# A fused attention and feed-forward kernel: the first batch worked by pair of heads, and a new order of loads and steps in the first two blocks

## The chip, the cores and the metric

The kernel runs on one core of one Trainium2 chip. The metric is the device time of one execution in microseconds (us). The core has five instruction queues that run side by side: TensorE (PE, the matrix unit; its loads of weights into the array are listed as PEld), VectorE (DVE), ScalarE (ACT), GpSimd (POOL) and SyncE (SP). SP, ACT and POOL can also start DMA transfers; here SP and POOL start nearly all of them. Each queue works strictly in the order in which the program wrote it, and waits at an instruction until the semaphores that it needs have come.

## What is computed

The reference, cut to what matters (8 batches, 8 heads, 576 rows, 64 columns a head; then a feed-forward layer of 512 by 2048 by 512 over all 4608 rows):

```python
q_s = softmax(q, over the 64 columns)
k_s = softmax(k, over the 576 rows)
kv  = einsum('bhsd,bhde', k_s transposed, v)       # 64 x 64 a head
x   = einsum('bhsd,bhde->bhse', q_s, kv)           # rows of 512 = 8 heads x 64
h   = x @ w_in                                     # 512 -> 2048
g   = where(h > 0, h, exp(min(h, 0)) - 1)
out = g @ w_out                                    # 2048 -> 512
```

## The kernel before

The feed-forward layer is most of the work. It goes batch by batch (a *block* j, 0 to 7, of 512 of the batch's 576 rows; a ninth block holds the 64 rows left over of all batches), and in each block over 16 *steps* c, one for each 128 columns of the hidden layer. A step has four matmuls of the hidden product (line 912, one for each pair of heads kc), the ELU on ACT, POOL and DVE (lines 892 to 896 and 925), and four matmuls of the output product (line 933). The output product of a step comes three steps later (`LAG`). Both products take their weights from SBUF (`W1S`, `W2S`), into which POOL loads them piece by piece in the first block; a word `w2:6:9` loads chunks 6 to 8 of `w_out`.

Everything else is woven into this by hand. For batch 0 the list `START` is worked off before block 0 begins. For batches 1 and later the work of batch j+1 stands in the tables `FIRST` (during block 0), `SECOND` (block 1) and `LATER`. A table has for each step three strings of words: after the hidden product, after the output product, and after the ELU of that step. Each word appends instructions to the queues of its engines in this order, so the order of the words is the order in every queue. The words that matter here:

- `load:Q:0:1` loads a pair of heads (a slot of 288 KB) of q of batch 0; in `START` the last field may name the queue. `load:K:1:M` loads all four slots of k of the next batch.
- `kmax` (DVE, four instructions a slot, line 326), `kturn` (PE, 331), `kacross` (DVE, 337 or 358), `diag` (ACT, 368) find the column maxima of k. For batch 0 `kraw` (PE, 513) copies k into PSUM and `kmin` (PE, 524) subtracts the maximum there, and `kexp` (ACT, 538 and 533) takes the exponential from there. `kspread` and `copy` do for batch 1 what `kmin` does.
- `qmax` (DVE, 672), `qsub` (679), `qexp` (ACT, 684), `qsum` (DVE, 689 and 691) and `qmul` (708) make the softmax of q; `qsub` and `qmul` run on POOL unless the word says `dve`.
- `pturn` (PE, 766 or 744) transposes it into a PSUM bank and `pwide` (ACT, 788) copies it to `QT`.
- `vconv` converts v to bf16, `kv` (PE, 560) makes k's product with v, `kfac` (614 to 629) scales it into `MB`; `att` (PE, 805) makes a pair's rows of x, and `xc` (814 or 812) copies them to `XT`, from which the hidden product reads. From batch 2 on `flat` and `xflat` (827, 855) do this in six cuts.
- `h` in `START` starts part of the hidden product of steps 0 to 3 early; `warm` runs matmuls whose result nobody reads; `hold` makes SP wait for the hidden product.

`AT` says which of the eight PSUM banks each word of batch 0 uses. A word that writes a bank waits until its last reader is done. In the kernel before, the tail of batch 0 goes by halves: `qmul:A`, `pturn:A`, `kv:A` and so on are two pairs of heads at a time, and the first part of the hidden product can be started for pairs 0 and 1 alone, since `h` and line 888 split a step's four matmuls in two and two.

Of the kernel before, what the change touches and what calls it, by code (L numbers as in the profile page):

```python
# [15 lines left out]
R = 4  # L16
SM = 128 * R
# [103 lines left out]
class Gen:  # L121
# [421 lines left out]
    def vconv_first(self, part, en="act"):  # L543

        P = "AB".index(part)
        vv = self.VR[0][:, 2 * P * QN:2 * (P + 1) * QN, :].rearrange("p (u r) d -> p u r d", u=2)
        out = self.VF[:, :, 2 * P:2 * P + 2, 0:64].rearrange("p r s d -> p s r d")
        self.copy(en, out, vv, self.firstkeys("V", part), [f"VF{part}"])

    def kv_first(self, part, bank):  # L550

        pe, P = self.E["pe"], "AB".index(part)

        def mm():
# [653 lines left out]
```

## Time and profile before

| | |
|---|---|
| three runs | 309.95, 310.0, 309.95 us; median 309.95 |
| span of the profiled execution, first to last instruction | 308.1 us |
| median of the runs less this span | 1.85 us (309.95 - 308.1) |
| start of the first hidden product, of the first output product | 19.88 us, 24.47 us |
| start of block 1, of block 2 | 54.66 us, 87.78 us |
| granted TensorE clock, mean | 1.000 |

The profiled execution's own time is not listed apart from its span; what lies around the span is taken as the 1.85 us above. The profile is one execution; times in it are in microseconds from the first instruction. A row of the timeline has the start, the time to the end of the last of the merged instructions, engine, line of the kernel, operation, output and inputs, shapes, how many, and in square brackets how long the engine had been idle and what ended that. A row of the groups has the busy time of the group and the mean nanoseconds of one instruction, then the idle time before them. A row of the windows has a stretch and its length, and for each engine the busy time and the number of instructions. A row of the waits has who waited for whom, the sum, how often, and the longest.

### The profile page before, as it was taken

The page shows a single profiled execution, that of the slowest core. Times are in us where ns is not written, and L with a number is a line of the kernel's source. Part 1 is how long each engine was busy: PE and PEld are TensorE (multiplying, and loading weights), DVE is VectorE, ACT ScalarE, POOL GpSimd, SP SyncE. Part 2 cuts the span into 40 slices and gives each one's busy share as a digit, 9 for nine tenths or more (in the row PEclk, how much of TensorE's full clock was granted, in tenths as well). Part 3 has the DMA queues.
Part 4 walks back from the last instruction along what each step waited for, and adds up shares of the span by engine and source line. Part 5 has one row for each costly group of instructions (what it writes and reads, how often), then busy time and mean ns, then how long its engine had stood idle before and what let it go on. Part 6 is the DMA issues. An engine that isn't in the chain of part 4 may idle for free.

```text
span 308.1 us, 4839 instructions
## 1 busy us (share of the span) xinstructions
PE 297.6 (97%) x1733; PEld 240.1 (78%) x1733; DVE 235.0 (76%) x400; ACT 192.9 (63%) x358; POOL 171.3 (56%) x215
## 2 busy tenths in 40 slices
PE   7789899999999999999999999999999999999995
PEld 4467677788878888888888888888888888888884
DVE  6988978979959897999889988998895353335442
ACT  2678975577559784877587758775877543334432
POOL 2968873686436743786278637863686333333440
PEclk9999999999999999999999999999999999999999
DMA  7999999985708993768475846590512030003004
GB/s 261 393 340 364 372 345 257 273 253 145 191 3 246 261 251 105 223 122 231 133 217 144 208 143 209 146 198 3 172 23 57 2 136 0 0 2 136 0 0 136
DMA packets 60584, 51.63 MB, mean 168 GB/s; under 512 B 26897, under 2 KB 50705, under 8 KB 60561
## 3 DMA queue, kind: packets, MB, share of 16 engines
q1 hardware_dynamic: 52960, 41.23, 47.7%
q0 software_dynamic: 6400, 8.39, 10.5%
q10 hardware_dynamic: 1200, 1.72, 2.0%
q8 instruction: 13, 0.21, 0.3%
q14 instruction: 11, 0.08, 0.1%
HBM read 38.27 MB, written 9.45 MB: 155 GB/s over the span
## 4 chain that ended last, share of the span: by engine, by line
PE 85%; DMA 6%; POOL 4%; ACT 2%; DVE 2%; issue 1%
PE bank L933 40%; PE bank L912 40%; DMA W2S<-in_moe_w_out_dram 5%; PE bank L827 2%; POOL W1S L255 1%; PE bank L598 1%; DMA QR<-in_q_dram 1%; POOL QR L679 1%; POOL QS L708 1%; PE bank L805 1%; DVE KT L326 1%; DVE QF L672 0%; PE bank L560 0%; ACT ES L895 0%; ACT ES L893 0%
## 5 line engine op out<-in xcount | busy, mean ns | idle before, releaser
L933 PE MATMUL bank<-W2S,GT 128*128 128x512 f32 x572 | 153.4, 391 | 1.4 <-DMA W2S<-in_moe_w_out_dram 1.2
L896 POOL TENSOR_SCALAR ES<-ES 128x512 f32<-128x512 f32 (+1 forms) x130 | 85.8, 662 | 117.3 <-ACT ES L895 117.3
L912 PE MATMUL bank<-XT,W1S 128*128 128x512 f32 x512 | 138.4, 392 | 0.5 <-issue 0.3
L925 DVE SCALAR_TENSOR_TENSOR GT<-bank,ES 128x512 fp32r<-128x512 f32 (+1 forms) x130 | 87.9, 681 | 54.4 <-PE bank L912 40.6
L933 PEld LDWEIGHTS bank<-W2S,GT 128*128 128x128 f32 x572 | 106.3, 188 | 23.6 <-DMA W2S<-in_moe_w_out_dram 1.6
L895 ACT ACTIVATE ES<-bank 128x512 f32<-128x512 f32 (+1 forms) x130 | 76.0, 592 | 70.9 <-PE bank L912 70.7
L912 PEld LDWEIGHTS bank<-XT,W1S 128*128 128x128 f32 x512 | 94.1, 188 | 19.9 <-ACT XT L814 0.9
L679 POOL TENSOR_TENSOR QR<-QR,QM 128x512 f32<-128x512 f32 (+1 forms) x21 | 24.9, 1187 | 0.6 <-DVE QM L672 0.5
L684 ACT ACTIVATE QR<-QR 128x1024 f32<-128x1024 f32 (+3 forms) x19 | 19.0, 1006 | 3.1 <-DVE QR L679 3.1
L855 ACT ACTIVATE XT<-bank 128x320 fp32r<-128x320 f32 (+1 forms) x30 | 15.0, 501 | 9.4 <-PE bank L827 9.3
L689 DVE TENSOR_REDUCE QZ<-QR 128x16 f32<-128x1024 f32 (+1 forms) x14 | 18.8, 1343 | 0.6 <-ACT QR L684 0.6
L672 DVE TENSOR_REDUCE QM<-QR 128x16 f32<-128x1024 f32 (+1 forms) x14 | 18.8, 1342 | 0.0
L912 PE MATMUL bank<-XTR,W1S 128*128 128x512 f32 x64 | 16.6, 389 | 0.0
L438 DVE TENSOR_TENSOR KR<-KR,NB 128x512 f32<-128x512 f32 x16 | 14.6, 938 | 0.0
L623 ACT ACTIVATE MB<-bank,KZ 64x64 fp32r<-64x64 f32 x44 | 10.1, 302 | 7.0 <-DVE KZ L614 6.9
L387 DVE TRANSPOSE_TENSOR_REDUCE KM<-KR 128x32 f32<-128x1024 f32 x12 | 14.4, 1226 | 0.0
L857 POOL CAST QT<-QW 128x1024 fp32r<-128x1024 f16 x12 | 12.5, 1039 | 2.9 <-DMA QW<-QS 2.9
L912 PEld LDWEIGHTS bank<-XTR,W1S 128*128 128x128 f32 x64 | 12.0, 188 | 2.5
L892 ACT ACTIVATE ES<-bank 128x512 f32<-128x512 f32 x15 | 8.9, 594 | 7.9 <-PE bank L912 7.9
L827 PE MATMUL bank<-QT,MB 128*128 128x320 f32 (+1 forms) x48 | 12.5, 300 | 0.7 <-ACT XT L855 0.7
L708 POOL TENSOR_TENSOR QS<-QR,QI 128x1024 f16<-128x1024 f32 (+1 forms) x7 | 12.5, 1783 | 0.4 <-DVE QI L691 0.4
L484 ACT ACTIVATE EK<-KR 128x1024 bf16<-128x1024 f32 x12 | 12.6, 1050 | 0.0
(108 smaller groups left out, 262.8 us busy)
## 6 DMA issues: line engine op xcount, KB each, us to landing
out_dram<-OSB SPq DMA_DIRECT2D x30, 256.0 KB, 2.7
KR<-in_k_dram SPq DMA_DIRECT2D x6, 1024.0 KB, 7.7
VR<-in_v_dram SPq DMA_DIRECT2D x6, 1024.0 KB, 6.3
QR<-in_q_dram SPq DMA_DIRECT2D x5, 1024.0 KB, 8.0
KR<-in_k_dram SPq DMA_DIRECT2D x8, 288.0 KB, 6.1
VR<-in_v_dram SPq DMA_DIRECT2D x8, 288.0 KB, 6.6
W1S<-in_moe_w_in_dram POOLq DMA_DIRECT2D x3, 768.0 KB, 9.2
QR<-in_q_dram SPq DMA_DIRECT2D x4, 512.0 KB, 11.2
```

The costliest lines, as they stand in the source:

```text
L672: self.op("dve", lambda: v.tensor_reduce(m, QR, AX.X, ALU.max), self.qkeys(b, part), self.qstat("QM", b, part))
L679: self.op(en, lambda: e.tensor_tensor(QR, QR, m, ALU.subtract), keys + self.qstat("QM", b, part), self.qown(b, part))
L684: self.op("act", lambda: a.activation(QR, QR, AF.Exp), keys, self.qown(b, part))
L689: self.op("dve", lambda: v.tensor_reduce(z, QR, AX.X, ALU.add), self.qkeys(b, part), self.qstat("QZ", b, part))
L708: self.op(en, lambda: e.tensor_tensor(out, QR, z, ALU.mult), keys + self.qstat("QI", b, part), [f"QS{x}" for x in cells])
L827: last = pe.matmul(self.bank[bank][:, a - c0:b - c0], self.MB[f][:, :, :].rearrange("p u d -> p (u d)"), self.QT[:, f, a - f * S:b - f * S ...
L855: self.op("act", lambda: e.activation(out, src, AF.Copy), reads, writes)
L895: self.op("act", lambda: a.activation(ES[:, x], ps[:, x], AF.Exp), [f"bank{bank}"], keys + mark)
L896: self.op("gp", lambda: g.tensor_scalar(ES[:, x], ES[:, x], -1.0, 1.0, ALU.add, ALU.mult), keys, keys)
L912: return pe.matmul(ps, self.W1S[:, kc, c * 128:(c + 1) * 128], x[:, kc, 0:SM], start=(kc == 0), stop=(kc == 3))
L925: self.op("dve", lambda: v.scalar_tensor_tensor(out[:, x], *how), [f"bank{bank}"] + eks + (["FINE"] if n < FINE else []), keys)
L933: return pe.matmul(self.bank[OB[t]][:, :], self.GT[n % NG][:, t * 128:(t + 1) * 128], self.W2S[:, c, :], start=(c == 0), stop=(c == NCH - ...
```

## The change

Four things, in one edit.

1. From `qmul` on, batch 0 goes by single pair of heads. `vconv`, `kv`, `kfac`, `pturn`, `pwide` and the reads of `att` now take a slot number; each of the four `kv` and `pturn` has an entry of its own in `AT`, and `QT`, `KZ` and the converted v are tracked by slot. No instruction computes more or less; two-slot instructions become two of half the size.
2. The hidden product of steps 0 to 3 is written out matmul by matmul in `START`, so that each waits for one pair only, and block 0 begins with all of it issued.
3. `START`, `FIRST` and `SECOND` have a new order, and several words another engine. Of the loads, slot 3 of k and of q of batch 0 and then `w2:0:2` and `w1:0:4` are started by POOL at its beginning; v comes in the order 0, 1, 2, 3; the rows left over of q of batch 1 move from `START` to step 5, v of batch 1 from step 6 to step 10, k and q of batch 2 to step 11.
4. Of the eleven matmuls of `warm`, the first five stay.

```diff
-AT = {"rawA": 0, "rawA2": 1, "rawB": 7, "rawB2": 4, "rawS": 3, "rawT": 2,
-      "kturnA": 4, "kturnB": 5, "kvA": 6, "kvB": 4, "pturnA": 5, "pturnB": 5,
-      "att0": 6, "att1": 2, "att2": 3, "att3": 4, "clip": (1, 2, 4, 6, 8, 10, 11, 17, 21, 30, 32, 33, 37, 42, 44)}
-START = ("load:Q:0:1 load:K:0:0 load:K:0:1 warm:1:7 warm:4:7 qmax:1 warm:2:4 load:Q:0:3 qsub:1:dve "
-         "load:Q:0:0 kmax:0 warm:3:5 load:K:0:2 kraw:A qexp:1 kmax:1 load:K:0:3 kturn:A load:V:0:1 "
-         "qmax:0 kraw:S qsum:1 qsub:0:gp kacross:A load:Q:0:2 kmax:3 kraw:B kmax:2 kmax2:R "
-         "load:V:0:0 w1:1:4 w1:0:1 diag:act:A qmax:2 kmin:S qexp:0 kraw:T kturn:B w2:0:2 qmax:3 "
-         "w1:4:6 kacross:B kexp:S vconv:A:act kmin:A qsub:2:gp qsub:3:gp diag:act:B w2:2:3 qsum:0 kmin:B "
-         "kexp:A load:V:0:3 kmin:T qexp:2 qmul:A:dve qsum:2 load:V:0:2 qexp:3 w1:6:9 "
-         "qsum:3 vconv:B:gp load:K:1:M qmul:2:gp kexp:B kexp:T kv:A kfac:A:dve pturn:A kv:B "
-         "pwide:A:act kfac:B:act warm:1:3 att:1 att:0 qmul:3:gp pturn:B xc:1:dve xc:0 h:2:4 "
-         "pwide:B:act w2:3:4 att:2 att:3 xc:2 load:Q:1:A load:Q:1:R w2:4:6 h:0:2 xc:3 kmax2:AB ")
+AT = {"rawA": 3, "rawA2": 5, "rawB": 7, "rawB2": 1, "rawS": 7, "rawT": 5, "kturnA": 2, "kturnB": 6,
+      "kv0": 0, "kv1": 1, "kv2": 4, "kv3": 0, "pturn0": 6, "pturn1": 5, "pturn2": 7, "pturn3": 1,
+      "att0": 6, "att1": 3, "att2": 2, "att3": 4,
+      "clip": (1, 2, 4, 6, 8, 10, 11, 17, 21, 30, 32, 33, 37, 42, 44)}
+START = ("load:K:0:1 load:K:0:3:gp load:K:0:0 warm:5:2 kmax:1 load:Q:0:0 load:K:0:2 kmax:0 load:Q:0:2 qmax:0 kraw:A "
+         "kturn:A kraw:S load:Q:0:3:gp w2:0:2 kacross:A diag:act:A kmin:A load:Q:0:1 kmax:2 kexp:A load:V:0:0 "
+         "kmin:S kraw:T qmax:2 kmax:3 w1:0:4 qsub:2:gp kturn:B qmax:1 qsub:0:gp kacross:B kexp:S qexp:2 qexp:0 "
+         "diag:act:B kraw:B qmax:3 load:V:0:1 kmin:B qsub:1:gp vconv:0:gp qsum:0 kmin:T qsub:3:gp qexp:1 "
+         "vconv:1:act qsum:2 load:V:0:2 kv:0 qmul:2:gp qsum:1 qmul:1:gp qmul:0:dve kexp:B kfac:0:dve kv:1 "
+         "qexp:3 qsum:3 load:V:0:3 vconv:3:act load:K:1:M pturn:0 pturn:2 kexp:T kv:3 vconv:2:act w1:4:6 "
+         "pwide:0:act pturn:1 pwide:2:dve qmul:3:gp kfac:1:dve kv:2 pwide:1:act att:0 pturn:3 kfac:3:dve "
+         "xc:0:act att:1 pwide:3:act kfac:2:dve h:0:0:1 kmax2:AB w2:2:3 h:0:3:4 att:2 w2:3:4 att:3 xc:1:act "
+         "h:0:1:2 h:1:1:2 load:Q:1:A xc:2:act h:1:0:1 w1:6:9 h:0:2:3 h:2:0:1 xc:3:act h:3:0:1 h:1:2:3 h:2:1:2 "
+         "h:3:1:2 h:2:2:3 h:1:3:4 h:3:2:3 h:2:3:4 h:3:3:4 ")
 FIRST = {
-    0: ("qmax:A ksub:R:dve", "", "qsub:0:dve"),
-    1: ("w1:13:14", "w1:9:12", "qsub:1:dve"),
-    2: ("", "qmax0:R", "w2:6:9"),
-    3: ("hold qexp:A", "load:Q:1:B:act", ""),
-    4: ("w1:12:13", "w2:9:13", "load:K:1:R qsum:A qsub0:R:dve"),
-    5: ("w1:14:16", "kturn", "kacross vconv:R qmax:C"),
-    6: ("", "qmul:A hold", "load:V:1:RAB"),
-    7: ("qexp0:R", "", "diag qsub:2:dve"),
-    8: ("qsub:D", "kspread load:K:2:MR copy ksub:1 qsum0:R", "qexp:C qmulr0:dve ksub:0 qsum:C"),
-    9: ("pturn:A", "", "ksub:3 kexp:R qmul:B:dve pwide:A:act"),
-    10: ("", "pturn0:R pwide0:R:act", "ksub:2:dve vconv:A:gp"),
-    11: ("rest0 rcopy0:act", "kexp:A", ""),
-    12: ("pturn:B w2:15:16", "pwide:B:act load:Q:2:ABR", "w2:13:15"),
-    13: ("kv:A vconv:B:dve", "kfac:A:dve", "kexp:B peak2:B att:0 xc:0"),
-    14: ("kv:B kfac:B:dve peak2:R qmulr:gp", "att:1 peak2:A", "join2 turn:R xc:1"),
-    15: ("att:3", "xc:3", "att:2 load:V:2:MR xc:2 kout2"),
+    0: ("", "", ""),
+    1: ("w2:4:6 w1:9:12 qmax0:R", "", ""),
+    2: ("qmax:A w2:6:9", "", ""),
+    3: ("qsub:1:dve hold", "", ""),
+    4: ("", "load:Q:1:B:act qsub:0:gp", ""),
+    5: ("qexp:A w1:12:13 w2:9:13", "kturn load:Q:1:R kacross diag", ""),
+    6: ("", "qsum:A qmul:A:dve kspread", "copy qsub0:R:gp"),
+    7: ("w1:13:14 qexp0:R qsum0:R", "qmax:C qmulr0:gp pturn:A w1:14:16 qsub:D:dve", "pwide:A:act qsub:2:gp"),
+    8: ("", "ksub:0 pturn0:R", "pwide0:R:act qexp:C ksub:1:dve"),
+    9: ("rest0", "qsum:C", "hold"),
+    10: ("rcopy0:act qmulr:dve load:V:1:RAB turn:R", "kexp:A", "qmul:B:gp ksub:3:dve"),
+    11: ("load:K:2:MR load:Q:2:ABR ksub:2:dve vconv:A:gp", "", ""),
+    12: ("pturn:B", "pwide:B:act", "w2:15:16"),
+    13: ("kv:A kfac:A:dve", "w2:13:15 att:0 kexp:B vconv:B:dve xc:0", ""),
+    14: ("kv:B kfac:B:act", "att:1 peak2:B xc:1", ""),
+    15: ("att:2 peak2:A", "xc:2 att:3 load:V:2:MR xc:3 peak2:R", "join2 kout2"),
 }
 SECOND = {
-    0: ("qmax:C qsub:D", "", "qmax:A"),
-    1: ("", "qsub:1 wide0:R:dve", ""),
-    2: ("", "qsub:0 load:K:2:MR", ""),
-    3: ("kin", "qsub:2 qexp:A", "qsum:A vconv:A:gp"),
-    4: ("", "", "ksub:A"),
-    5: ("rest0", "qexp:C", "peak2:B"),
-    6: ("ksub:3:dve rcopy0:act vconv:B", "ksub:R:dve", "load:Q:2:MR"),
-    7: ("", "kexp:A", "ksub:2 kexp:R"),
-    8: ("qmul:1 qsum:C qmul:0:dve", "vconv:R", "kexp:B qmulr:dve"),
-    9: ("turn:A", "qmul:B:dve", ""),
-    10: ("peak2:R wide:A:gp kv:AB", "", ""),
-    11: ("kfac:AB:dve", "turn:R turn:B qmax2:A", ""),
-    12: ("peak2:A wide:R:act", "flat:0", "xflat:0:act"),
-    13: ("flat:1", "xflat:1:act", ""),
-    14: ("join2", "flat:2 xflat:2:act kout2", "wide:B:gp load:V:2:MR"),
-    15: ("flat:3", "xflat:3:dve flat:4", "xflat:4:act flat:5 xflat:5:act xrest:dve"),
+    0: ("qmax:A wide0:R:act qmax:C", "", "qsub:2"),
+    1: ("", "", "kin"),
+    2: ("load:K:2:MR", "", "qsub:0 ksub:2:dve"),
+    3: ("", "qsub:1 ksub:R:dve qsub:D:dve vconv:B", ""),
+    4: ("vconv:R", "", "qexp:A ksub:A qsum:A"),
+    5: ("peak2:A qexp:C ksub:3:gp", "", ""),
+    6: ("", "", "vconv:A:act qmul:0:gp"),
+    7: ("rest0", "kexp:B", "kexp:A qmul:1 qsum:C rcopy0:dve kexp:R qmulr:dve"),
+    8: ("", "load:Q:2:MR", ""),
+    9: ("peak2:B", "", ""),
+    10: ("load:V:2:MR kv:AB turn:A qmul:B:gp wide:A:act kfac:AB:act turn:R turn:B wide:R:act", "peak2:R", ""),
+    11: ("", "", "flat:0 xflat:0:act"),
+    12: ("", "qmax2:A", "flat:1 xflat:1:act"),
+    13: ("wide:B:dve", "flat:2", "xflat:2:act"),
+    14: ("flat:5 xflat:5:dve join2", "flat:3 xflat:3:act", ""),
+    15: ("flat:4", "xflat:4:act xrest:act kout2", ""),
 }
...
     def kv_first(self, part, bank):
-        pe, P = self.E["pe"], "AB".index(part)
+        pe, xs = self.E["pe"], self.slots(part)
...
-            for x in range(2 * P, 2 * P + 2):
+            for x in xs:
...
-        self.hidden_mm(j, c, range(2, 4) if n < EARLY else range(4))
+        self.hidden_mm(j, c, () if n < EARLY else range(4))
...
-                for c in range(int(args[0]), int(args[1])):
-                    self.hidden_mm(0, c, range(2))
+                for c in range(int(args[1]), int(args[2])):
+                    self.hidden_mm(0, c, (int(args[0]),))
```

The other edits pass the slot numbers through: `vconv_first`, `kv_fac`, `qturn_slots`, `qwide_first`, and the keys by which reads of `QT` and of the converted v are tracked.

More of the change, by code (lines that the diff above doesn't have):

```diff
@@ L148, in need, with cells, slots @@
                 know[s] = n
+    def cells(self, key):
+        if key in ("QTA", "QTB"):
+            return [f"QT{x}" for x in self.slots(key[-1])]
+        if key in ("VFA", "VFB"):
+            return [f"VC{x}" for x in self.slots(key[-1])]
+        return [key]
+    def slots(self, part):
+        return {"A": (0, 1), "B": (2, 3)}.get(part) or (int(part),)
     def op(self, en, fn, reads=(), writes=(), dma=None):
         own = f"s_{en}"
+        reads, writes = ([x for k in keys for x in self.cells(k)] for keys in (reads, writes))
         evs = []
@@ L610, in kv_fac @@
         v = self.E["dve"]
-        hs = ["AB".index(x) for x in part]
-        f0, f1 = 2 * hs[0], 2 * hs[-1] + 2
+        fs = [f for x in part for f in self.slots(x)]
+        f0, f1 = fs[0], fs[-1] + 1
         ps = self.bank[bank][:, 0:4 * VW].rearrange("p (f c) -> p f c", f=4)
         self.op("dve", lambda: v.reciprocal(self.KZ[:, f0:f1], ps[:, f0:f1, 64]),
-                [f"bank{bank}"], [f"KZ{hh}" for hh in hs])
+                [f"bank{bank}"], [f"KZ{f}" for f in fs])
         a = self.E["act"]
@@ L618, in kv_fac @@
             sl, keys = slice(64 * u, 64 * u + 64), [f"MB{f}u{u}" for f in range(f0, f1)]
-            reads = [f"bank{bank}"] + [f"KZ{hh}" for hh in hs]
+            reads = [f"bank{bank}"] + [f"KZ{f}" for f in fs]
             if en == "act":
@@ L755, in qturn_slots @@
         else:
-            hh = "AB".index(part)
-            v = self.QS[hh][:, :, :, :].rearrange("p r h d -> p (r h) d").rearrange("p (r u) d -> p r u d", u=2)
-            src, reads = [v[:, r, :, :] for r in range(QF)], [f"QS{2 * hh + x}" for x in range(2)]
+            xs = self.slots(part)
+            v = self.QS[xs[0] // 2][:, :, :, :].rearrange("p r h d -> p (r h) d").rearrange("p (r u) d -> p r u d", u=2)
+            src, reads = [v[:, r, :, :] for r in range(QF)], [f"QS{x}" for x in xs]
         n = len(src)
+        us = (0, 1) if part == "R" else [x % 2 for x in xs]
         def mm():
             for i, x in enumerate(src):
-                for k in range(4):
-                    u, h = k // 2, slice(64 * (k % 2), 64 * (k % 2) + 64)
-                    o = 64 * (2 * i + u if part == "R" else u * n + i)
-                    last = pe.transpose(ps[h, o:o + 64], x[h, u, :], self.ID16[h, h])
+                for u in us:
+                    for k in range(2):
+                        h = slice(64 * k, 64 * k + 64)
+                        o = 64 * (2 * i + u if part == "R" else u * n + i)
+                        last = pe.transpose(ps[h, o:o + 64], x[h, u, :], self.ID16[h, h])
             return last
@@ L831, in attend_flat @@
         fs = [x // 2 for x in VISIT[v]]
-        self.op("pe", mm, [f"MB{f}u{u}" for f in fs for u in range(2)] + sorted({f"QT{'AB'[f // 2]}" for f in fs}) +
+        self.op("pe", mm, [f"MB{f}u{u}" for f in fs for u in range(2)] + sorted({f"QT{f}" for f in fs}) +
                 (["QTR"] if v else []), [f"bank{bank}"])
```

28 lines of the change are left out of this document (15 added, 13 removed).

## The prediction

> **What bounds the kernel now.** First the page: engines, and the chain that ended last.
>
> ```profile
> span 308.1 us, 4839 instructions
> PE 297.6 (97%) x1733; PEld 240.1 (78%) x1733; DVE 235.0 (76%) x400; ACT 192.9 (63%) x358; POOL 171.3 (56%) x215
> PE 85%; DMA 6%; POOL 4%; ACT 2%; DVE 2%; issue 1%
> ```
>
> PE is busy 97% of the span and makes 85% of the chain. The number of its instructions changes by six idle matmuls only, so the change can gain only where PE waits or has not begun. The waits of PE from 20 to 100 us, then three stretches (block 0 from step 4; block 1; block 3, whose table is not touched):
>
> ```profile
> PE bank L933 <- DMA W2S<-in_moe_w_out_dram: 1.2, 2, 0.9
> PE bank L827 <- ACT XT L855: 0.7, 1, 0.7
> PE bank L912 <- ACT XT L814: 0.2, 1, 0.2
> 25.50:54.66 29.16, 27.92 (x206) 21.32 (x204) 25.04 (x41) 21.02 (x36) 20.17 (x22) 1.00 1.19 323
> 54.66:87.78 33.12, 32.20 (x181) 26.09 (x180) 29.79 (x53) 21.32 (x36) 21.58 (x24) 1.00 0.71 200
> 119.15:150.34 31.19, 31.19 (x177) 25.64 (x176) 27.63 (x45) 21.85 (x43) 19.41 (x24) 1.00 0.67 176
> ```
>
> Little is to be had. Block 0 loses 1.2 us to late pieces of `w_out`. Block 1 is 33.12 - 31.19 = 1.93 us longer than block 3; its four extra matmuls (181 against 177) are `rest0`, some 0.5, so about 1.4 is loss, with the 0.7 and 0.2 in it. The other place is the prologue. Its tail, in the timeline:
>
> ```profile
> 16.82 2.06 POOL L708 TENSOR_TENSOR QS<-QR,QF 128x512 f16<-128x512 f32 x2
> 19.67 1.02 ACT L788 ACTIVATE QT<-bank 128x1024 fp32r<-128x1024 f16 x1
> 21.31 1.09 ACT L814 ACTIVATE XT<-bank 128x512 fp32r<-128x512 f32 x2 [0.62 <-PE bank L805]
> 21.34 2.98 PE L912 MATMUL bank<-XT,W1S 128*128 128x512 f32 x12
> 24.47 1.20 PE L933 MATMUL bank<-W2S,GT 128*128 128x512 f32 x4 [0.15 <-DVE GT L925]
> ```
>
> POOL's `qmul` of pairs 2 and 3 ends at 18.88; transpose, `pwide`, `att`, `xc` follow one after the other until 22.40; the twelve matmuls left run till 24.3; the first output product starts at 24.47.
>
> **The prologue after.** Durations, from the groups of the first 24.4 us (busy, mean ns):
>
> ```profile
> L672 DVE TENSOR_REDUCE QF<-QR 128x8 f32<-128x512 f32 x4 | 2.6, 681 | 1.0 <-DMA QR<-in_q_dram 1.0
> L326 DVE TENSOR_TENSOR KT<-KR 128x256 f32<-128x256 f32 x4 | 1.8, 440 | 0.0
> L326 DVE TENSOR_TENSOR KT<-KT 128x128 f32<-128x128 f32 x6 | 1.8, 292 | 0.2
> L326 DVE TENSOR_TENSOR KA<-KT,KR 128x64 f32<-128x64 f32 x4 | 0.9, 226 | 0.1
> L679 POOL TENSOR_TENSOR QR<-QR,QF 128x512 f32<-128x512 f32 x3 | 3.1, 1063 | 5.8 <-DVE QF L672 5.8
> L684 ACT ACTIVATE QR<-QR 128x512 f32<-128x512 f32 x4 | 2.4, 623 | 3.1 <-DVE QR L679 3.1
> L538 ACT ACTIVATE EK<-bank 128x512 bf16<-128x512 f32 x4 | 2.1, 586 | 0.0
> L368 ACT ACTIVATE DG<-ID,NM 128x128 fp32r<-128x128 f32 x4 | 1.4, 393 | 3.8 <-DVE NM L337 3.8
> L814 ACT ACTIVATE XT<-bank 128x512 fp32r<-128x512 f32 x3 | 1.7, 595 | 0.6 <-PE bank L805 0.6
> L855 ACT ACTIVATE VB<-VR 128x1152 bf16<-128x1152 f32 x1 | 1.2, 1157 | 0.0
> L513 PE MATMUL bank<-KR,ID 128*128 128x512 f32 x8 | 3.9, 611 | 1.0 <-DMA KR<-in_k_dram 1.0
> L255 POOL DMA_DIRECT2D W1S<-in_moe_w_in_dram x5 | 4.0, 806 | 0.0
> DMA to landing us min/median/max: 2.9/5.2/6.6
> ```
>
> The last row is of the twelve loads of batch 0: issued from 0.73 to 6.05, the first landed at 3.65, the last at 12.7. Queues in order, after the change: DVE starts `kmax` of slot 1 at 3.65; two slots at 0.44 + 0.29 and twice 0.23 = 1.19, `qmax:0` 0.68, `kacross` about 0.25, `kmax:2` 1.19, `qmax:2` 0.68: with short waits, about 8.9 to 9.0. POOL takes `qsub` of 2 and 0, 1.06 each: 11.1. ACT takes `qexp:0` until 11.7, and from there it is ACT that sets the end, without a gap: `diag` 0.79, `qexp:1` and `qexp:3` 1.25, two `vconv` before and one after `kexp:T` at half of 1.157 (1.74), `kexp:B` 1.17, `kexp:T` 0.28, three `pwide` at half of 1.02 (1.53), four `xc` 2.38: 9.1, so the last `xc` ends at 20.8. Halving gains since pair 3's `pwide` and `att` no longer hold pair 0 to 2; it does not shorten ACT's sum.
>
> One wait is added on this list: `vconv:3` wants slot 3 of v at about 15.3. V is now behind weights. The two stretches 8 to 13 and 13.6 to 18 us of the DMA view:
>
> ```profile
> DMA packets 974, 1.99 MB, mean 399 GB/s; under 512 B 109, under 2 KB 109, under 8 KB 974
> L255 POOL DMA_DIRECT2D W1S<-in_moe_w_in_dram x1: 967/967/967, 9.2 to 9.2; - x1
> DMA to landing us min/median/max: 9.2/9.2/9.2
> q0 software_dynamic: 574, 0.81, 60.2%
> q1 hardware_dynamic: 597, 0.78, 59.2%
> ```
>
> SP's queue (q1) alone moves 399 GB/s, a 0.295 MB slot each 0.74 us. POOL's (q0), once it has work, takes half: 0.78 MB in 4.4 us is left to SP, a slot each 1.66. POOL's load issued at 9.2 moved nothing before 13, so at least 3.8 us of delay: slot 3 of k, issued by POOL at about 2.5, begins at 6.3 or later and lands near 8.3, before `kmax:3` at 9.0. By 6.3 to 6.8 SP's queue has landed four to five of its ten slots; the rest at 1.66 puts slot 3 of v at 15.1 to 16.5. I take a wait of 0.6 (ends 0 and 2.0, the upper if POOL's share is larger than the row's). Behind it in ACT's queue stand all four `pwide` and `xc`. So the last `xc` ends at 21.4. The four issues of POOL cost 4 x 0.81 from 2.4 to 5.7, hidden, since POOL has nothing until 9.0 (in the row above it idles 5.8 us). `w1:0:4` is 1.05 MB behind 1.1 MB on the same queue and lands at about 18, ahead of the first use at 19.
>
> Then PE runs the ninth to last matmul of steps 0 to 3 at 21.5; nine at a spacing of 0.228 (a step of eight in 1.82) make 2.05: first output product at 23.55 to 23.7 against 24.47. **Gain 0.8** (ends -0.6 and 1.4). DVE's `kmax2` still ends at 22.8 as before and the first ELU is not held by it.
>
> Five warm matmuls remain instead of ten at the start:
>
> ```profile
> L1093 PE MATMUL bank<-GT,ONES x10: 389/628/793, 1.7 to 5.4; 128*128 128x512 f32 x10
> ```
>
> Most take 628 ns, the last 389: PE ran at half rate until about 5. Afterwards five end at 4.2 and `kraw:A` follows when slots 0 and 1 of k are there, about 4.4: a hole of 0.2. I take no cost. The Trainium skill, "TensorE: Matmul & The Clock Gate", Part 1: The HAM clock gate, says that the array starts at half clock and is released by a window of about 3.4 us of sustained activity; the trace agrees (1.67 to about 5.05), and no run here shows how much activity is enough. That is a rival below.
>
> **Block 0 after.** The 1.2 us for `w_out` go: v of batch 1 (1.18 MB), k and q of batch 2, that shared the DMA from 34 us, now come after step 9, and `w2:6:9` is issued at about 25. Taken: **+1.2**. What is late next is DVE. `qmul:A` is now DVE's and `pturn:A` stands in step 7 instead of 9. Rows of before:
>
> ```profile
> 22.76 1.21 DVE L672 TENSOR_REDUCE QM<-QR 128x16 f32<-128x1024 f32 x1
> 24.66 0.68 DVE L679 TENSOR_TENSOR QR<-QR,QM 128x512 f32<-128x512 f32 x1
> 26.46 0.41 DVE L672 TENSOR_REDUCE QF<-QR 128x4 f32<-128x256 f32 x1
> 29.50 1.21 DVE L689 TENSOR_REDUCE QZ<-QR 128x16 f32<-128x1024 f32 x1
> 31.09 1.94 POOL L708 TENSOR_TENSOR QS<-QR,QI 128x1024 f16<-128x1024 f32 x1 [0.38 <-DVE QI L691]
> 33.12 1.27 ACT L368 ACTIVATE DG<-ID,NM 128x128 fp32r<-128x128 f32 x4
> 40.17 1.77 DVE L708 TENSOR_TENSOR QS<-QR,QI 128x1024 f16<-128x1024 f32 x1
> ```
>
> DVE from 23.1 (first ELU) without a gap: six ELUs at 0.68 (the first in two halves, 0.76) 4.2, `qmax0:R` 0.41, `qmax:A` 1.21, `qsub:1` 0.68, `kacross` about the same 0.41, `qsum:A` 1.46 with its reciprocal, `qmul:A` 1.77: 10.1, so 33.2. PE comes to `pturn:A` after nine groups of four matmuls (8.2) and small ones: 32.3. It waits 0.7 or so; behind it all of step 8 is queued. `kspread` waits some 0.2 for `diag` (1.27, behind `qexp:A`). On the same count DVE's `qsum:C` ends at 41.3, POOL's `qmul:B` (1.94) at 43.2, and PE is at `pturn:B` at 42.9: 0.35. Sum **-1.25** (ends 0, if DVE keeps up as before where it never held PE, and -4 if every such place slips by another microsecond).
>
> **Block 1 after.** Before, three `flat` in step 15 go through one bank in turn, which is where the 0.7 lies; after, one stands in each of steps 11 to 13 and 15 and two in 14. The 1.4 goes but for 0.1 at `xc:3` and about 0.3 at `flat:0`, which waits for eight scalings on ACT behind `wide:A`: **+1.0** (ends 0 and 1.3). Blocks 2 to 8 are unchanged.
>
> Sum: 0.8 + 1.2 - 1.25 + 1.0 = 1.75 of the span of 308.1; the median of the runs is 1.85 above that span, and I take this to stay: 309.95 - 1.75 = **308.2**.
>
> **The rivals.**
> - *No new wait on DVE and POOL.* For it: no wait of PE on DVE in block 0 before. Against: DVE's list above has no gap. Gain 0.8 + 1.2 + 1.4 = 3.4: 306.5.
> - *The pairs bring nothing*, since ACT's sum is the same and v comes late: prologue 0; 309.0.
> - *The array stays at half clock* through `kraw:A`: its four passes take 1.95 (3.9 for eight) at full clock and up to 3.9 at half, and end at 8.3 instead of 6.35; `kturn:A` is queued behind, and DVE's `kacross`, which waits for it, holds `kmax:2`. Up to 1.9 is lost: 309.95 - 1.75 + 1.9 = 310.1. For it: half the warm matmuls. Against: the array has hardly a hole until 6.3. By the skill's window the outcome hangs on one window of 3.4 us.
> - *DVE becomes the bound of block 0 and the start of block 1* (slower). Place: steps 5 to 9 and 15 to step 2 of block 1, where `peak2`, `join2` and both `qmax` now stand together before an ELU. A bank of the hidden product is wanted three steps later, 5.4 us less product, exponential and ELU: some 2.5 us of slack. Beyond that each microsecond of DVE is one of PE. If `qmul:A`, `pturn:B` and the ELU of step 0 each come 1 us later than counted, 3.0 more are lost: 309.95 - 1.75 + 3.0 = 311.2. It decides from 1.75 of further lateness on.
>
> **Chances.** Forecast 0.38, nothing on DVE 0.16, pairs nothing 0.10, half clock 0.12, DVE 0.24. The bound is 0.2%, 0.62 us, about what a measurement here can tell from no change: faster 0.38 + 0.16 + 0.10 = 0.64, within 0.12, slower 0.24. The range reaches from the best ends (1.4 + 1.2 + 1.3 = 3.9: 306.0) to 311.0, near the slower rival; the forecast's own is 307.0 to 309.3.
>
> **What would show it.** First output product before 24 us, and ACT without gaps from 11 us: the prologue right. No wait on W2S in block 0. A wait of PE line 766 or 744 on DVE's or POOL's QS: the new wait; its size decides. Block 1 near 32. Matmuls of line 513 near 600 ns from 5 us on: the clock was up. Wrong if slot 3 of k lands after 10, or if the waits of PE in block 0 exceed 3 us.

## The result and the profile after

The changed kernel takes 320.87 us (median of 4 runs, 319.55 to 322.51), the kernel before 309.98 in the same rounds: ratio 1.0351, 95% interval 1.0312 to 1.0389. It is slower by 10.9 us; the forecast was 1.75 us faster, with a range that ended at 311.0. The profiled execution took 320.63 us with a span of 318.8, so what lies around the span stayed at 1.8.

The head of the page after, and the same three stretches as in the prediction: block 0 from step 4, block 1, block 3 (start:end and length, then busy time of PE, PEld, DVE, ACT and POOL, granted clock, DMA share, GB/s).

```profile
span 318.8 us, 4844 instructions
PE 300.7 (94%) x1727; PEld 239.7 (75%) x1727; DVE 240.4 (75%) x402; ACT 198.9 (62%) x373; POOL 170.8 (54%) x216
27.23:56.74 29.51, 28.36 (x206) 21.11 (x204) 27.52 (x38) 21.86 (x40) 18.48 (x22) 1.00 1.09 299
56.74:98.65 41.91, 34.92 (x181) 26.73 (x180) 31.70 (x52) 25.48 (x47) 19.34 (x21) 0.96 0.68 169
129.83:161.00 31.17, 31.17 (x177) 25.64 (x176) 27.62 (x45) 21.84 (x43) 19.48 (x24) 1.00 0.67 176
```

Block 0 from step 4 on lost 0.35 (29.51 against 29.16), no more than one execution differs from another (28.36 to 29.50 in the kernel before and in e7, e10 and e15 below, whose lists are the same up to block 1); block 3, which nobody touched, is the same. Block 1 takes 41.91 instead of 33.12: **8.8 of the 10.7 us** by which the span grew. Before step 4 of block 0 lie 1.7 more (27.23 against 25.50); the later blocks give 0.2 back. PE's waits from 20 to 100 us name the new holders:

```profile
PE bank L930 <- DVE GT L943: 4.3, 1, 4.3
PE bank L951 <- ACT OSB L960: 2.1, 1, 2.1
PE bank L784 <- DVE MB L645: 0.8, 1, 0.8
```

The waits for `w_out` (1.2 before) are gone, as forecast; one wait for DVE and one for ACT, both in block 1, take their place (the third, for `MB`, is in the prologue). PE's timeline there (start, length, engine, line, operation, count; in brackets the wait):

```profile
62.88 1.09 PE L930 MATMUL bank<-XT,W1S 128*128 128x512 f32 x4
66.08 1.23 PE L951 MATMUL bank<-W2S,GT 128*128 128x512 f32 x4 [2.12 <-ACT OSB L960]
67.15 1.08 PE L930 MATMUL bank<-XT,W1S 128*128 128x512 f32 x4
...
68.97 1.07 PE L930 MATMUL bank<-XT,W1S 128*128 128x512 f32 x4
...
75.25 1.80 PE L930 MATMUL bank<-XT,W1S 128*128 128x512 f32 x4 [4.31 <-DVE GT L943]
...
78.56 1.30 PE L930 MATMUL bank<-XT,W1S 128*128 128x512 f32 x4
```

Read the distances of the hidden products (L930), 1.82 in a quiet step: 62.88 to 67.15 is 4.27 (ACT), 68.97 to 75.25 is 6.28 (DVE), and 75.25 to 78.56 is 3.31 although nothing waits, since four matmuls take 1.8 us instead of 1.07. The granted clock says why:

```profile
72.00:75.50 3.50, 0.24 (x1) 0.25 (x2) 3.47 (x4) 0.87 (x1) 1.78 (x2) 1.00 0.93 265
75.60:79.00 3.40, 3.40 (x10) 2.62 (x9) 3.37 (x6) 1.85 (x3) 1.23 (x2) 0.50 0.30 83
```

After 4.3 us of standing still the array ran at half clock for 3.4 us. So the 8.8 are about 2.5 behind ACT, 4.5 behind DVE and 1.7 of half clock (the last counted from the two steps after the wait).

What ACT did, and what DVE and POOL did, in that stretch (ACTq is a DMA that ACT issues):

```profile
59.30 0.43 ACTq L431 DMA_DIRECT2D kmax_scratch<-KU  x1
64.55 0.35 ACTq L437 DMA_DIRECT2D NB<-kmax_scratch  x1
64.95 0.60 ACT L913 ACTIVATE ES<-bank 128x512 f32<-128x512 f32 x1 [2.97 <-DMA kmax_scratch<-KU]
```

```profile
68.28 1.12 DVE L452 TENSOR_TENSOR KR<-KR,NB 128x512 f32<-128x512 f32 x1 [1.31 <-DMA NB<-kmax_scratch]
69.32 3.34 DVE L458 TENSOR_TENSOR KR<-KR,NB 64x256 f32<-64x256 f32 x2
72.69 1.91 DVE L695 TENSOR_TENSOR QR<-QR,QM 128x768 f32<-128x768 f32 x1
74.52 1.28 DVE L943 SCALAR_TENSOR_TENSOR GT<-bank,ES 128x512 fp32r<-128x512 f32 x2
```

```profile
69.85 3.93 POOL L452 TENSOR_TENSOR KR<-KR,NB 128x1024 f32<-128x1024 f32 x2
```

The maxima of k make a round trip through DRAM: `kout` writes them, `kin` reads them back into `NB`. `kin`, now at the end of step 1, is an instruction of ACT and waits there for `kout` to land; behind it stood the exponential and the eviction `OSB` (2.97 idle). Before, `kin` stood in step 3, 5.9 us behind `kout`, and ACT did not wait for it:

```profile
55.88 0.36 ACTq L417 DMA_DIRECT2D kmax_scratch<-KU  x1
...
61.76 0.35 ACTq L423 DMA_DIRECT2D NB<-kmax_scratch  x1
```

```profile
69.46 0.86 DVE L444 TENSOR_TENSOR KR<-KR,NB 64x256 f32<-64x256 f32 x2
```

Then `ksub:2`, `ksub:R` and `qsub:D` on DVE. The first waits 1.31 us for `NB`, that is, for `kin`. The two `ksub:R` took 0.86 before and 3.34 now, beside POOL's `ksub:A` and `ksub:3`; before, `ksub:A` ran on POOL at 65.61 to 68.01, while DVE had reductions and ELUs. The ELUs that PE wants stand behind them.

The prologue: first output product at 26.20 (24.47 before).

```profile
4.50 3.38 PE L527 MATMUL bank<-KR,ID 128*128 128x512 f32 x4 [0.33 <-DMA KR<-in_k_dram]
```

```profile
8.02 0.29 DVE L351 TENSOR_REDUCE NM<-bank 128x2 f32<-128x128 f32 x1 [1.21 <-PE bank L345]
...
10.45 2.00 DVE L340 TENSOR_TENSOR KT<-KT 128x128 f32<-128x128 f32 x2
```

```profile
10.18 2.19 POOL L695 TENSOR_TENSOR QR<-QR,QF 128x512 f32<-128x512 f32 x2 [4.97 <-DVE QF L688]
```

```profile
20.50 0.44 PE L784 MATMUL bank<-ID,QS 64*64 64x64 f16 x16 [0.79 <-DVE MB L645]
...
26.20 0.96 PE L951 MATMUL bank<-W2S,GT 128*128 128x512 f32 x3 [0.25 <-DVE GT L943]
```

`kraw:A` ran at half rate, by the length of its matmuls (3.38 against 1.96; the column of the granted clock shows 1.00 there), `kacross:A` came at 8.02 after 1.21 of waiting, and of `kmax:3` two steps took 2.00 instead of 0.55 beside POOL's `qsub`.

### The profile page after: what moved, and what is told of

The parts are those of the page before. It is cut to its first block, busy times and chain, and to the rows that moved or that the text cites. A ratio compares the mean times of both kernels' runs of the same rounds, so it can differ in the third digit from the quotient of the medians.

```text
span 318.8 us, 4844 instructions
## 1 busy us (share of the span) xinstructions
PE 300.7 (94%) x1727; PEld 239.7 (75%) x1727; DVE 240.4 (75%) x402; ACT 198.9 (62%) x373; POOL 170.8 (54%) x216
## 4 chain that ended last, share of the span: by engine, by line
PE 82%; DVE 9%; DMA 6%; issue 1%; ACT 1%; POOL 0%; SPq 0%; DVEq 0%
PE bank L930 38%; PE bank L951 37%; DMA KR<-in_k_dram 3%; PE bank L845 2%; DMA kmax_scratch<-KU 2%; DVE GT L943 1%; PE bank L614 1%; DMA NB<-kmax_scratch 1%; PE bank L527 1%; DVE KT L340 1%; DVE KR L458 1%; DVE QF L705 1%; DVE KM L401 1%; DVE QR L695 1%; ACT MB L639 1%
## 5 line engine op out<-in xcount | busy, mean ns | idle before, releaser
L930 PE MATMUL bank<-XT,W1S 128*128 128x512 f32 x512 | 139.4, 395 | 4.3 <-DVE GT L943 4.3
L930 PEld LDWEIGHTS bank<-XT,W1S 128*128 128x128 f32 x512 | 94.3, 189 | 24.2 <-DVE GT L943 4.9
L930 PE MATMUL bank<-XTR,W1S 128*128 128x512 f32 x64 | 16.6, 389 | 0.0
L639 ACT ACTIVATE MB<-bank,KZ 64x64 fp32r<-64x64 f32 x52 | 11.9, 302 | 7.1 <-DVE KZ L630 6.9
L724 POOL TENSOR_TENSOR QS<-QR,QI 128x1024 f16<-128x1024 f32 (+1 forms) x9 | 15.4, 1712 | 1.2 <-DVE QI L707 1.2
L930 PEld LDWEIGHTS bank<-XTR,W1S 128*128 128x128 f32 x64 | 12.0, 188 | 2.5
L596 ACT ACTIVATE VB<-VR 128x1024 bf16<-128x1024 f32 x12 | 12.6, 1054 | 0.0
L845 PEld LDWEIGHTS bank<-QT,MB 128*128 128x128 f32 x48 | 9.0, 187 | 4.0 <-ACT XT L873 1.0
```

Of the source, the lines that this page charges most:

```text
L724: self.op(en, lambda: e.tensor_tensor(out, QR, z, ALU.mult), keys + self.qstat("QI", b, part), [f"QS{x}" for x in cells])
L845: last = pe.matmul(self.bank[bank][:, a - c0:b - c0], self.MB[f][:, :, :].rearrange("p u d -> p (u d)"), self.QT[:, f, a - f * S:b - f * S ...
L930: return pe.matmul(ps, self.W1S[:, kc, c * 128:(c + 1) * 128], x[:, kc, 0:SM], start=(kc == 0), stop=(kc == 3))
```

## The experiments

Ratios are to the kernel before on the same chip, whose median was 310.1 to 310.3 in every group. "P0" is the first output product.

**The three tables, one by one and two together.** Each of the first three is the kernel before or after with one table exchanged; two loads (`load:Q:1:R`, `w2:4:6`) go where the old tables have them.

```diff
 e1: START new, FIRST new, SECOND of before
 e5: START new, FIRST and SECOND of before
 e6: kernel before with FIRST new
 e7: kernel before with SECOND new
```

> Only the list before block 0 is the new one (with the pairs' banks); the two tables for blocks 0 and 1 are those of before. If the prologue loses by itself what it loses in the changed kernel: first output product at 26.2 to 27.2 us instead of 24.47, block 0 and 1 at 30 and 33 us, total 311.7 to 313. If the prologue's lateness is given back inside block 0 (the loads of block 0 have more time, so the wait for w_out goes): 310.5 to 311. By the prediction's term (0.8 gained): 309.2.

> Only the table of block 0 is the new one. By the prediction's terms for block 0 (1.2 of w_out gained, 1.25 lost on DVE) it stays at 310.0 within 0.6, without a wait of PE on W2S. If the late loads of batch 2's k alone harm block 1 even with the old table there: block 1 near 35 us instead of 33.1, total 311.5 to 312.5.

> Only the table of block 1 is the new one; k of batch 2 is loaded as early as before. Theory A (the new table is slow by itself: kin in step 1 behind kout, ACT held, both qmax, three ksub and qsub before an ELU): block 1 40 us or more, a clock drop near its middle, total 315 to 318. Theory C (it is slow only because block 0's table brings k of batch 2 late, so that join2 and kout come 3 us later): kout issued near 56, kin lands before the ksub, block 1 32 to 34, total 309 to 311.

Measured: START alone (e5) 312.09 (1.0063, 1.0038 to 1.0089), FIRST alone (e6) 313.47 (1.0111, 1.0088 to 1.0134), SECOND alone (e7) 317.09 (1.0222, 1.0194 to 1.025). Block 1 takes 33.08 in e5 and 35.06 in e6; no wait for W2S is listed in either. Each part is slower by itself: 2.0, 3.4 and 7.0 us, 12.4 together against 10.9. The run e1, for which was expected

> The changed kernel with the table SECOND of before (START, FIRST and the code as changed). Block 1 took 41.91 us in the changed kernel and 33.12 before. Theory A (the new order of SECOND costs it: ACT's queue waits 2.97 us for k's maxima to come back through DRAM at the word kin, two steps earlier than before; DVE then waits for them and its ELU comes late; PE idles 4.3 us and its clock halves for 3.4 us): block 1 back to 33 to 34, the whole 312 to 313.5, no stretch of half clock after the prologue. Rival C (what FIRST leaves behind, k's maxima sent only at 59.3 because the loads of batch 2 came late, costs the same with either table): block 1 at 39 or more, the whole 318 or more.

gave 315.11 (1.0156, 1.0135 to 1.0178), block 1 34.96 us, one above theory A's range (e14 below shows why). In e7 k of batch 2 is loaded as early as before and `kout` leaves at 56.77, 1.22 behind the start of block 1 as in the kernel before, yet block 1 takes 39.87: theory C falls as the main cause, theory A stands. Block 1 of e7, its waits of PE, and DVE's rows:

```profile
55.55:95.42 39.87, 34.44 (x182) 26.84 (x180) 31.25 (x50) 25.39 (x47) 19.37 (x21) 0.96 0.62 166
```

```profile
PE bank L912 <- DVE GT L925: 4.3, 1, 4.3
PE bank L933 <- ACT OSB L942: 0.8, 1, 0.8
```

```profile
66.67 3.34 DVE L444 TENSOR_TENSOR KR<-KR,NB 64x256 f32<-64x256 f32 x2
70.04 1.91 DVE L679 TENSOR_TENSOR QR<-QR,QM 128x768 f32<-128x768 f32 x1
```

The same 4.3, the same 3.34 and 1.91.

**Block 1: DVE beside POOL.**

```diff
-    4: ("vconv:R", "", "qexp:A ksub:A qsum:A"),
-    5: ("peak2:A qexp:C ksub:3:gp", "", ""),
+    4: ("vconv:R", "", "qexp:A ksub:A:dve qsum:A"),
+    5: ("peak2:A qexp:C ksub:3:dve", "", ""),
```

> The changed kernel with the subtraction of k's maxima for heads 0 to 3 and pair 3 on DVE instead of POOL, so that POOL runs nothing long beside ksub:R and qsub:D. Theory D (DVE is slowed by POOL's tensor_tensor at the same time): the two ksub:R take 0.9 us together instead of 3.3, qsub:D about 1.0 instead of 1.9; although DVE gets some 2 us of work more, PE's longest wait on DVE's GT falls from 4.3 to under 2.5 us, the drop of the clock goes, block 1 takes 37 to 39 us instead of 41.9, total 316 to 318. Rival (DVE's list is simply too long there, or the wait for NB decides): ksub:R stays long or the wait grows with DVE's work, block 1 42 to 44, total 321 to 323.

Measured: 317.45 (1.0227, 1.0192 to 1.0262), 3.4 less than the changed kernel by the medians, block 1 37.98.

```profile
57.09:95.07 37.98, 33.66 (x182) 25.53 (x181) 29.36 (x52) 25.54 (x47) 15.95 (x19) 1.00 0.76 187
```

```profile
69.32 1.28 DVE L458 TENSOR_TENSOR KR<-KR,NB 64x256 f32<-64x256 f32 x2
70.63 0.96 DVE L695 TENSOR_TENSOR QR<-QR,QM 128x768 f32<-128x768 f32 x1
```

```profile
PE bank L930 <- DVE GT L943: 2.3, 2, 1.3
PE bank L951 <- ACT OSB L960: 1.9, 1, 1.9
```

DVE does 1.87 us of work more (1.22 and 0.65 for what it took over from POOL), and its list is *earlier*: 3.34 and 1.91 became 1.28 and 0.96, the longest wait of PE for DVE fell from 4.3 to 1.3, and the clock of block 1 stayed at 1.00. Theory D is shown. In the changed kernel the second `ksub:R` alone took 2.48 and ended at 72.66, just behind POOL's first long operation (69.85 to 72.38), and `qsub:D` ran until about 0.8 behind its second one (73.78): DVE stood still as long as POOL ran. The wait for ACT's `OSB` is untouched by this edit: a second cause.

**Block 1: `kin` early.** The kernel before with one word moved, and the changed kernel with `kin` and two subtractions moved back:

```diff
 e10 (before): "kin" from the start of step 3 to the end of step 1
 e2 (after):
-    1: ("", "", "kin"),
-    2: ("load:K:2:MR", "", "qsub:0 ksub:2:dve"),
-    3: ("", "qsub:1 ksub:R:dve qsub:D:dve vconv:B", ""),
-    6: ("", "", "vconv:A:act qmul:0:gp"),
+    1: ("", "", ""),
+    2: ("load:K:2:MR", "", "qsub:0"),
+    3: ("kin", "qsub:1 qsub:D:dve vconv:B", ""),
+    6: ("ksub:2:dve", "ksub:R:dve", "vconv:A:act qmul:0:gp"),
```

> The kernel before with one word moved: kin from step 3 to the end of step 1 of block 1, where the changed kernel has it. ACT then stands at kin until kout has landed (about 61 us): an idle of about 2 us on ACT and a late exponential and eviction behind it. Theory K (this wait is a large part of the block's 8.8 us): PE waits 1 to 2 us on ACT's OSB or GT, block 1 34 to 35.5 us, total 311 to 312.5. Rival (the later products take it up, since the slack between product and bank is some 2.5 us): block 1 within 0.3 of 33.1, total 310 within 0.6.

> The changed kernel with three words of SECOND moved: kin from step 1 to step 3 as before, and the two subtractions on DVE that read its result (ksub:2, ksub:R) from steps 2 and 3 to step 6. Theory A (the wait at kin and what hangs on it is the loss of block 1): block 1 at 33.5 to 35, the whole 312.5 to 314.5, no wait of PE over 1 us on ACT or DVE. Rival B (the rest of the new order, DVE's qsub and POOL's ksub and qsub side by side, is slow by itself): waits of PE on DVE's ELU stay at 2 us or more in all, the whole 316.5 or more.

Measured: e10 311.10 (1.0033, 1.0011 to 1.0056), block 1 34.05, and a wait that the kernel before does not have in this block:

```profile
PE bank L933 <- ACT OSB L942: 0.7, 1, 0.7
```

So `kin` in step 1 costs 0.9 us there, and 2.1 to 2.5 in the changed kernel. There `kout` leaves 2.56 behind the start of block 1 (59.30), against 1.22 before (55.88). e2 gave 317.54 (1.0214, 1.0178 to 1.0251), block 1 36.92 against 41.91, no wait for `OSB` and, in the profiled execution, no half clock. Yet the total is as its rival B had it, not theory A: waits for DVE remain (2.2 in all, the longest of them shown), block 0 from step 4 took 31.21 (the other two waits for DVE, 0.36 and 0.66, lie in it; the rest of the 1.7 above the changed kernel's is not explained), and 1.9 of a new wait is for `MB`, whose scalings `kfac:AB` the new table puts on ACT:

```profile
PE bank L845 <- ACT MB L639: 1.9, 1, 1.9
PE bank L930 <- DVE GT L943: 1.2, 1, 1.2
```

**What else the new table of block 1 costs.** e7 with `kin` and all subtractions of k's maxima where the kernel before has them (`kin` at the start of step 3, `ksub:A` on POOL in step 4, the others on DVE in step 6).

> The run with the new table of block 1 alone (317.1), with kin and the subtractions of k's maxima put back where the kernel before has them (kin at the start of step 3, heads 0 to 3 on POOL in step 4, the rest on DVE in step 6). If the early kin, with what it puts side by side on DVE and POOL, is all that the table loses: block 1 33 to 34 us instead of 39.9, total 310 to 311. If the rest (both qmax in a row, qsub:D and the quarters of k's maxima in new places) has a share of its own: block 1 35 to 37, total 312 to 314.

Measured: 313.17 (1.0087, 1.0059 to 1.0114), block 1 36.10: 3.8 of the 6.8 us that this table adds to block 1 are `kin` with the subtractions; 3.0 are the rest.

```profile
PE bank L912 <- DVE GT L925: 2.0, 1, 2.0
PE bank L827 <- ACT MB L623: 1.1, 1, 1.1
71.83 2.01 DVE L444 TENSOR_TENSOR KR<-KR,NB 64x256 f32<-64x256 f32 x2
72.36 1.20 POOL L708 TENSOR_TENSOR QS<-QR,QI 128x512 f16<-128x512 f32 x1
```

The wait of 2.0 for DVE looks like the same effect: in their old place the subtractions now run beside POOL's `qmul` (69.89 to 71.37 and 72.36 to 73.56), and `ksub:R` takes 2.01 instead of 0.86. No run moves these two apart. The wait of 1.1 is for `kfac:AB` on ACT.

**Block 0's late loads.** The changed kernel with k of batch 2 issued in step 8 again instead of 11 and v of batch 1 at the end of step 8; e14 has the old SECOND with it.

> The changed kernel with k of batch 2 issued again in step 8 of block 0 (before turn:R and v of batch 1, which goes to the end of step 8). Theory C: the maxima of k are ready 3 to 5 us earlier, kout is issued near 56 to 57, the wait for kin goes, the drop of the clock with it; block 1 35 to 37 instead of 41.9, total 314 to 316. Theory A: block 1 stays at 40 or more, total 319 to 321. If the loads now collide with pieces of w_out: a wait on W2S of about 1 us comes back in block 0.

> The changed kernel with the old table for block 1 and k of batch 2 issued again in step 8 of block 0, v of batch 1 at its end. Theory C (what the new table of block 0 costs lies in block 1, since k and q of batch 2 come late for the maxima): block 1 33 to 33.6 us instead of the 35.0 that it took with the old table and late loads; total 313 to 314 instead of 315.1. Rival (the cost is of DVE's queue in steps 13 to 15 whatever the loads do): block 1 stays at 34.6 to 35.2.

Measured: e8 320.59 (1.0306, 1.0248 to 1.0363), block 1 39.50 instead of 41.91, but the first output product comes 2.0 later in its profiled execution, which has half clock from 11.9 to 18.7 us (more on this below), so that the total shows nothing. The wait for `OSB` stays (1.7), against what theory C expected. e14 314.24 (1.0114, 1.0074 to 1.0155), block 1 33.30 against 34.96 in e1:

```profile
58.18:91.48 33.30, 32.61 (x181) 25.94 (x180) 29.90 (x53) 21.26 (x36) 22.16 (x24) 1.00 0.68 182
```

The late loads cost block 1 1.7 us, about half of FIRST's 3.4; with the old table and early loads block 1 is back within 0.2 of the kernel before. In total e14 is only 0.9 below e1, with intervals that overlap, since block 0 took 0.5 more there.

**The prologue.**

```diff
 e3 (after):  warm:5:2 -> warm:10:2
 e4 (before): without warm:2:4 and warm:3:5
 e13 (e5):    "qmax:2 kmax:3" -> "kmax:3 qmax:2"
```

> The changed kernel with ten warm matmuls at the start instead of five. Theory H (the array stayed at half clock until 7.34 us since the first 3.4 us were not busy enough; kraw:A took 3.38 instead of 1.96 us): full clock from about 5.0, kraw:A about 2 us long but begun at 5.6 instead of 4.5, kacross:A at about 7.9 instead of 8.0, so the whole within 0.5 us of the changed kernel, unless the ending at 7.34 was chance. Rival (five are as good, the moment of release comes from the window's phase and not from the warm matmuls): release at about 7.3 again.

> The kernel before with only its first five warm matmuls (and the one-instruction group late in the prologue), those after them left out. Theory H: the clock is released at about 7.3 instead of 5.03, kraw:A and what follows come 1 to 1.5 us later, and the first output product at 24.5 to 25.5: 310.0 to 311. Rival (release does not depend on them): release at about 5.0 and the time within 0.2 of before, or a little less.

> The run with the new list before block 0 alone, with one exchange: kmax:3 stands before qmax:2, so that DVE has done its two-input maxima of slot 3 before POOL starts qsub:2 and qsub:0. Theory L (the two-input operations of DVE stand still while POOL's tensor_tensor runs, and this is what the prologue loses): the steps of kmax:3 take 0.3 and 0.2 us again instead of 1.0 and 0.9, kacross:B comes 1 us or more earlier, first output product 0.8 to 1.4 us earlier than in that run, total 310.7 to 311.4. Theory H (the slow first matmuls and the late slot 2 of k set it, ACT is the end of the chain): first output product within 0.4 of that run, total 311.8 to 312.5.

Measured: e3 322.03 (1.038, 1.0351 to 1.0408), e4 310.01 (0.9992, 0.9976 to 1.0008). By the lengths of its matmuls the half rate at the start ended at 7.2 us with ten warm matmuls in e3 and at 7.3 with five in the changed kernel; in e4 it ended at 9.05 (before: 5.03), P0 moved only from 24.47 to 24.94, and the time not at all. So in these two executions ten warm matmuls in the new order ended the half rate no sooner than five. But with five, `kraw:A` takes 2.44 (e13) to 3.78 us (e2, e8) from one kernel's profile to the next, so that one profile each cannot tell their number from chance. e13: 311.54 (1.0029, 1.0011 to 1.0046) against e5's 312.09, between the ranges of its two theories, and the intervals overlap. `kmax:3` runs unhindered

```profile
10.18 0.55 DVE L340 TENSOR_TENSOR KT<-KT 128x128 f32<-128x128 f32 x2
```

but `qmax:2`, moved behind it, starts POOL at 11.67 instead of 10.15, ACT's `diag` for pairs 2 and 3 stands behind the exponentials that wait for POOL (14.28 against 13.51), and P0 is at 27.64 against 27.30. The two profiled executions also differ in `kraw:A` (2.44 against 3.36) and in the clock, here in e13 (1.00 in e5 over the same stretch):

```profile
15.75:19.15 3.40, 3.39 (x85) 2.94 (x86) 3.23 (x9) 3.40 (x8) 3.40 (x4) 0.50 1.11 395
```

So the 1.45 us that DVE stands still are real, and e13 does not decide what they cost. Half clock in the prologue also came with the new list, and no step of the forecast had it. Between 9 and 20 us a stretch of it stands in the profiles of e1, e3, e8, e13 and e14, five of the nine kernels with the new START, and in none of the eight with the old one. In e5 the three executions with a mean clock of 1.000 took 311.39 to 311.74, the three with 0.989 and 0.994 took 312.45 to 313.46; a stretch of 3.4 us at half clock lowers the mean over 310 us by about 0.0055, so these fit one and two stretches; where in the span they lay is not recorded. P0 lies at 26.20 to 28.20 in the nine profiles with the new START and at 24.47 to 25.40 in the eight with the old one, so one profile each does not rank small differences. What the rest of START's 2.0 us is made of stays open.

**Can the kernel before gain its waits?** `w2:6:9` ahead of `w1:13:14`; e12 moves one `flat` from step 15 to 14 as well.

> The kernel before with pieces 6 to 8 of w_out issued before piece 13 of w_in (the two change places between steps 1 and 2 of block 0). If the prediction's term of 1.2 for w_out holds by itself: no wait of PE on W2S in block 0, total 308.8 to 309.2. Rival (the wait only moves to the next late piece, or another engine is late next): 309.6 to 310.2.

> The same, and in block 1 pair 3's widening one step earlier and one flat more in step 14, so that two and not three stand in step 15: the prediction's loss of 0.7 at XT in step 15. If the term holds by itself: 0.5 to 0.7 below the run with w_out alone, 308.2 to 308.6. Rival (another exponential on ACT or the extra flat holds PE as long): equal to it within 0.3.

Measured: e11 312.22 (1.0044, 1.0012 to 1.0077), e12 312.54 (1.0061, 1.0037 to 1.0085): both slower, and e11 above both of its ranges. In e11 the wait became one of 2.3, later, with half clock behind it:

```profile
PE bank L933 <- DMA W2S<-in_moe_w_out_dram: 2.3, 1, 2.3
46.75:50.15 3.40, 3.40 (x31) 2.27 (x32) 0.00 (x0) 0.52 (x2) 0.00 (x0) 0.50 1.19 336
```

e12 has the same wait (2.4), without half clock in the profiled execution, and its second wait for `XT` only moved a step ahead (0.62 at 86.87 in step 14, beside 0.7 in step 15). No version found here beats the kernel before.

## Why the prediction was wrong

The step that failed is **"Block 1 after: +1.0"**. It looked at steps 11 to 15, and at `xc:3` just ahead of the block. Steps 11 to 15 hold no gain: from the hidden product of step 11 to the end of the block 11.15 us now, 11.17 before, since `flat:0` waits and the extra flat of step 14 give back what step 15 saves. And the new steps 0 to 7 lose 8.8, none of which stood in the sum: it put at nothing that DVE's subtractions stand still beside POOL's, and that ACT waits at `kin`.

- *The fourth rival* had DVE ahead of an ELU, but not the place: in steps 15 to 2 of block 1 no wait of PE for DVE is listed; its waits are in step 3 (ACT) and step 5 (DVE). And it counted lengths, not what runs beside them, and gave 3.0. DVE's subtractions standing still beside POOL's, with the half clock behind the wait, are 3.9 of the block (e9). The prediction charged every operation one length, whatever ran beside it. Its own rows held the sign: it took 1.77 for `qmul` of two pairs from 40.17 of the kernel before, where POOL's subtraction runs until 40.86. The same operation takes 1.21 at 75.10, and 1.22 as `qmul:A` in the changed kernel.
- *A moved wait was not charged.* `kin` moved from step 3 to step 1 and past the evictions in ACT's queue; what was queued behind it stood in no sum. It costs 0.9 us alone (e10) and 2.1 to 2.5 in the changed kernel.
- *Block 0, w_out: +1.2.* The waits are gone, also with FIRST alone (e6). With START alone they are gone too, though the loads stand as before: there block 0 begins 2.84 us later and `w2:6:9` is issued only 1.26 later (26.97 against 25.71). Block 0 from step 4 takes 27.49, that is 1.67 less than before.

```profile
28.34:55.83 27.49, 27.49 (x206) 21.24 (x205) 25.03 (x41) 19.96 (x34) 18.91 (x20) 1.00 1.13 310
```

- *Block 0, DVE: -1.25* had the right sign, and 29.51 against these 27.49 is -2.0, within the ends given. But PE does not wait for `QS` at either `pturn`, as was counted; its waits in block 0 are for `MB` (0.5 for DVE and 0.4 for ACT, ahead of `att` in steps 13 and 14) and 0.2 for ACT at `pturn:B`. That the size came near was in part luck. Late k also cost 1.7 in block 1 (e14), which no step priced.
- *Prologue: +0.8* came out as -1.7 in this pair of profiles. The 0.6 for v did not come (no engine waits for it), and slot 3 of k landed at about 7.2 (issued at 2.36, 4.8 to landing), ahead of the 8.3 that was counted. But `kraw:A` did stay at half rate, as the third rival had it, so that `kacross:A` waited 1.21, POOL began at 10.18 rather than 9.0, and `qexp:0` ended at 13.03 rather than 11.7. From there ACT's list was taken as gapless; it has gaps (0.64 for PE, which itself waits 0.79 for scalings on DVE, 20.50 above), and the last `xc` ended at 23.55 rather than 21.4. In the old order a half rate until 9.05 cost nothing (e4); what it costs in the new order was not separated.

On the clock, the Trainium skill, "TensorE: Matmul & The Clock Gate", Part 1, speaks of a window of about 3.4 us; the trace agrees: the half clock after the long wait lasted 3.4 us (75.6 to 79.0). On DVE and POOL, the Trainium skill, "SBUF — State Buffer", section "Who interferes with whom", says that a DVE instruction with two SBUF inputs contends with a GpSimd instruction that reads SBUF, and the page's section "SBUF: two separate sides" that whichever starts first holds the shared pair for its whole length. The trace agrees (3.34 beside POOL, 1.28 or 0.86 without, and the end 0.3 us behind that of POOL's first operation), and also where the page says that `tensor_reduce` does not contend: `qmax` kept 0.68 beside POOL (13.41 us). No step of the forecast used this page, and its sum lacked just this.

## What to carry to other kernels

When an operation is moved, write down what runs at that moment on the engine beside it, not only what is queued on its own: operations of DVE with both inputs in SBUF, as the subtractions here, and POOL's add up as if they were on one engine. If the same operation shows two lengths in the profile before, find out why before taking one. A DMA that waits is an instruction of the queue that issues it; moving it earlier moves its wait ahead of work that others need. And price a wait of PE of some 2 us and more with the half clock that may follow it; here it followed some of these waits and not others.

## What the runs showed of the hardware

- DVE's two-input `tensor_tensor` beside POOL's: two steps of `kmax` 2.00 instead of 0.55 us, the two 64x256 3.34 instead of 0.86, the 128x768 1.91 instead of 0.96. An ELU with one input in PSUM kept its 0.69 beside POOL's subtraction (65.74 in the kernel before).
- The half rate at the start ended between 5.0 and 9.05 us, by the lengths of the matmuls: at 7.2 with ten warm matmuls and at 7.3 with five in the new order. An end at 9.05 (e4) changed the time by less than its interval.
- Half clock came back for 3.4 us after waits of PE of 4.3 (the changed kernel, e7), 3.1 (e8), 2.3 (e11) and 1.75 us (e3), and not after waits of 2.9 (e3), 2.4 (e12), 2.1 (the changed kernel, at 66.08) or 1.9 and 1.3 (e9): the length of the wait alone does not decide. It also came between 9 and 20 us, in stretches of 3.4 or 6.8 us, in five of nine profiles with the new list before block 0.
